# A gated mix of linear attention and a GEGLU MLP: loads, sums and products put in another order in four places, and one tile for four short-lived buffers

## The chip, the cores and the metric

The kernel runs on one core of one Trainium2 chip. The metric is the time of one execution on the device in microseconds (us), taken as the median of several runs.

## The reference

With `S` = 2048 tokens, `D` = 576, 32 heads of 18 and `Df` = 4608:

```python
g = sigmoid((x * gate_w).sum(-1))                      # one gate for each token
q, k, v = split(x @ wqkv)                              # 32 heads
phi = lambda t: where(t > 0, t + 1, exp(t)) + 1e-6
kv = einsum("bhsd,bhse->bhde", phi(k), v)              # sums over all tokens
z  = phi(k).sum over tokens
a  = (phi(q) @ kv) / (phi(q) @ z + 1e-6) @ wo          # linear attention
b  = (gelu(x @ w_gate) * (x @ w_up)) @ w_down          # MLP
out = g * a + (1 - g) * b
```

All of it is fp32. The keys' states `kv` need every token before the first query can be used, and the MLP needs nothing of the attention.

## The kernel before, in words

TensorE (PE) takes an fp32 operand as a rounded high part and the rest, the low part; a product is the sum of three matmuls: high by high, high by low and low by high. ACT writes high parts (a copy into `fp32r`), DVE or GpSimd (POOL) write low parts (a subtraction). The order of the instructions on each engine is written out by hand: nothing is scheduled by a planner, and an engine takes its instructions strictly in that order. The program has three stages.

**Keys and values** (L160 to L415). `w_first` and `x_first` (L168 to L186) issue the first loads of the weights `wkv` and the tokens `xt`, on ACT's queue and on SP's (SyncE's). For each of 16 token tiles `t` and three chunks `c` of the columns, `proj_mm` (L196) issues 14 matmuls for the projection, and `kv_post` (L210) forms phi(k) and v from it. `kv_state` (L242) adds tile `t`'s part to the states: for each of five groups of heads one matmul with the high part of v (L248, 252 columns, 144 for the last group) and one with the low part (L250, 126 columns, 72 for the last), ten in all. In the loop at L379 the states of tile `t-2` follow chunk `c` = 0 of tile `t`.

**Mixing** (L400 to L675). The order is written as words, and `run` calls them one by one. A letter names a step, the digits its token block `b` (of 512 tokens) and group, tile or index. `Q` is a query projection (L433, 14 matmuls of 512 columns), `a` its activation, `h` and `d` the parts for the denominators and their matmul (L570), `r` the reciprocals of a block (L592: for each half one ACT copy L598, one DVE addition L599 and one DVE reciprocal L600, then DMAs that spread them over the partitions). `p` scales the queries of one token tile (L615 DVE, L616 ACT, L617 and L618 DVE), `m` multiplies them with the combined weights (L628, 28 matmuls of 288 columns into one of two PSUM pairs), and `e` scales the pair by the gate on ACT and stores it (L633, L635). `X` loads a chunk of the MLP's tokens (L641; chunks 1 and 2 from POOL's queue), `y` forms four sums of its quarters in place (L645 to L648, DVE), and `Y` splits them into parts (L652 ACT, L655 POOL, four subtractions). `W` loads a whole set of MLP weights. In the last of the words the MLP's first products begin: `G1`, `G6`, `G2`, `G7`, each 14 matmuls there, with `g` for what follows them.

**MLP** (from L682). It is a Winograd-Strassen product: seven products for each of gate (G1 to G7) and up (U1 to U7) instead of eight, on 2x2 blocks of 256 features and 1024 tokens, so 2 passes over the tokens by 18 feature blocks: 36 periods. One G or U is 7 matmuls of 512 columns (L690). The down products D (`unit`, L781) are 6 matmuls of 288 columns (L787), each reading one feature operand (h or hx: A11, A12, A22, S1 to S4, with a high and a low half), and E (`unit_out`) adds their results into `sums`. The table `ORDER` (L39) is the order of one period, and `emit` (L929) goes through it for every period `p`; a mark of +1 means that the step belongs to the period before, and @ that POOL does it. When the sums of a group of four token tiles are complete, `gated` (L774) multiplies them with one minus the gate and adds the attention's part: ACT L776, then POOL L777. The last period has no next one to hide under: its down products are formed directly, 12 matmuls for each of 8 token tiles (`down`, L981), in the order 4, 5, 6, 7, 0, 1, 2, 3, and `down_out` (L992) adds each to `sums` and stores it.

Four buffers of the MLP, `p1`, `u2`, `u3` and `e0`, are tiles of a pool `mid` (L675), opened after the pool `chunks` of X's tiles is closed, so that they lie on memory that chunks had. `p1` takes the copy (L703, ACT) of product G1's bank, that is, of PSUM.

Of the kernel before, what the change touches and what calls it, by code (L numbers as in the profile page):

```python
# [21 lines left out]
NG = 5  # L22
# [28 lines left out]
def tile_gated_mix(ctx, tc, xt, xs, wkv, wq, wo, wgu, wgt, wdn, cst, out):  # L51
# [124 lines left out]
    x_first(nc.sync, 0)  # L176
    w_first(nc.sync, 0, *cols[1])
    x_first(nc.sync, 1)
    w_first(nc.sync, 1, 0, KVC)
    x_first(nc.sync, 2)  # L180
# [14 lines left out]

    def proj_mm(t, c, out_t, ops):  # L196
        b, c0 = divmod(t * 128, BS)
        lo, n = CH[c]
        for k, (xa, i, r, rows) in enumerate(x_ops(b, c0, 128)):
            if k in ops:  # L200
                nc.tensor.matmul(out_t[:, :n], xa, kvw[i][:rows, r, lo:lo + n], start=(k == 0), stop=(k == 13))  # L201

    pk, vt = {}, {}
# [37 lines left out]

    def kv_state(t):  # L242
        p = pk.pop(t)[1]
        v = vt.pop(t)
        for g in range(NG):
            R, k = GR[g], slice(GO[g], GO[g] + GR[g])
            o = acc_a[:, g // 2, (g % 2) * 252:(g % 2 + 1) * 252] if g < 4 else acc_b[:, 0, :2 * R]
            nc.tensor.matmul(o, v[:, g * VW:g * VW + 128], p[:, :, k], start=(t == 0 and g in (0, 2, 4)),  # L248
                             stop=False, skip_group_check=True)
            nc.tensor.matmul(o[:R, :R], v[:, g * VW + 128:g * VW + 128 + R], p[:, 0, k], start=False,  # L250
                             stop=(t == NST - 1), skip_group_check=True)

# [126 lines left out]
    for t in range(2, NST):  # L379
        for c in range(3):  # L380
            ps = bank()
            proj_mm(t, c, ps, range(14))
            if c == (1 if t == 2 else 0):
                kv_state(t - 2)
            for part in (("k0",), ("k1", "s"), ("v",))[c]:
                kv_post(t, c, ps, part)
            do()
            if steps:
                steps.popleft()()
        if t == 3:  # L390
# [149 lines left out]
    def kw_load(g):  # L540
        kwr = kwr_of[g] = kwp.tile([128, D], F32, name="kwr", bufs=4)
        if g < 4:
            nc.sync.dma_start(kwr, kw_d[128 * g:128 * g + 128])
        else:
            for i in range(2):
                nc.sync.dma_start(kwr[64 * i:64 * i + 64], kw_d[512:])
# [32 lines left out]
    run("""  # L579
s Q24 a24 w1 i1 Q20 u z w2 i2 Q21 Q23 a21 o1 a20 h21 o2 w4 i4 f1 w0 i0 Q22 n f2 o4 a23 f4 h20 w3 i3 o0 Q30 f0  # L580
l1 l4 d20 v a22 o3 l0 f3 d21 Q33
    """)
# [75 lines left out]
    run("""  # L658
h22 d22 c1 Q32 l2 a30 h23 l3 d23 h24 X0 h30 d24 Q31 c4 a33 c2 r2 d30 a32 c0 a31 c3 h32 h31 Q01 a01 Q34 d31 h33
a34 Q00 p20 d32 Q04 h34 a00 d33 a04 p21 h00 m20 x Q02 y0 h01 d34 m21 Q03 r3 d00 h04 d01 a02 a03 h02 Q10 h03  # L660
d02 Q11 e20 d03 p23 m23 Y0 p22 a10 d04 e21 p31 m22 h10 e23 p30 X1 y1 r0 a11 m31 e31 Q14 e22 m30 Y1 a14 p33 h11
Q12 a12 d10 Q13 d11 e30 m33 p32 h12 d12 a13
    """)
# [254 lines left out]
    for word in ORDER.split():  # L918
# [3 lines left out]
        table.append((word[:-2] if shift else word, shift, nc.gpsimd if on_pool else nc.vector))  # L922
    assert sorted(name for name, _, _ in table) == sorted(ops)
    last_of = [[name for name, _, _ in table if name[0] == g][-1] for g in "GU"]

    done = {(name, 0) for name in ("G1", "gp1", "G6", "gu2", "G2", "gel0", "G7", "gu3")}
    after = deque()

    def emit(name, n, e):  # L929
# [62 lines left out]
    def down_out(t, turn, by_halves):  # L992
# [4 lines left out]
        else:  # L997
            nc.vector.scalar_tensor_tensor(a, pr[turn % 2][:, :, :288], gate[:, 1, st:st + 1], a, op0=mul, op1=add)
# [21 lines left out]
    for group in (order[:2],) + tuple((t,) for t in order[2:]):  # L1020
# [65 lines left out]
```

## Time and profile before

| | |
|---|---|
| time before, median of 3 runs | 1516.87 us (1516.15 to 1518.5) |
| the profiled execution, its own time | 1517.35 us |
| its span in the trace | 1515.6 us |
| outside the span | 1.75 us |
| busy share PE / DVE / POOL / ACT | 99% / 73% / 49% / 38% |
| mean granted clock of PE | 0.996 |

The span is the time from the first to the last recorded work; busy is the time in which an engine executes. Busy times of matmuls overlap by a little, since they are pipelined: a row's start and the next row's start are the safer pair. A row of a timeline gives the start, the busy time, the engine, the line and the operation, and in brackets the idle time ahead of it with what ended it. A row of the waits gives the engine's instruction, what it waited for, the total, the number of waits and the longest. A row of the windows gives the busy time of PE, PE's weight load, DVE, ACT and POOL with their instruction counts, then the granted clock (1.00 is full), the share of DMA time and GB/s.

### The profile page before, as it was taken

To read this page: it belongs to the slowest core of one execution; us is meant where nothing else is said; L and a number is where in the kernel's file an instruction comes from. 1 tells how busy PE (TensorE), PEld (TensorE's weight loads), DVE (VectorE), ACT (ScalarE), POOL (GpSimd) and SP (SyncE) were. 2 spreads that over 40 slices of the span, in tenths; PEclk is the share of its full clock that TensorE was granted. 3 is DMA by queue.
4 is the path that set the end of the run, shared out by engine and by line. 5 is a ranking of instruction groups with operands and counts; after the bars stand their busy time and mean duration, and the time that the engine had idled before them with its cause. 6 is when DMAs were issued, how large, how long until landed. Compare 5 with 4: busy or idle time off the path is not lost.

```text
span 1515.6 us, 21450 instructions
## 1 busy us (share of the span) xinstructions
PE 1497.4 (99%) x8181; PEld 1326.2 (88%) x8181; DVE 1107.5 (73%) x1690; ACT 577.6 (38%) x965; POOL 746.9 (49%) x710
## 2 busy tenths in 40 slices
PE   9999998999999999999999999999999999999998
PEld 8999888888888888888888888888888888888887
DVE  6534677378888888888878867777777777777776
ACT  6655755333434343434343323222222222222223
POOL 1473412177877877878867625233233232332323
PEclk9999999999999999999999999999999999999999
DMA  6676565656666766665566376334433344344441
GB/s 214 205 254 217 172 210 190 205 193 212 205 222 243 253 241 220 211 232 200 202 236 216 115 300 239 151 138 162 179 147 138 138 176 160 138 153 182 181 172 63
DMA packets 115748, 291.15 MB, mean 192 GB/s; under 512 B 6845, under 2 KB 87037, under 8 KB 105278
## 3 DMA queue, kind: packets, MB, share of 16 engines
q1 hardware_dynamic: 111834, 276.63, 51.7%
q10 hardware_dynamic: 3524, 11.06, 2.1%
q0 software_dynamic: 288, 2.10, 0.4%
q8 instruction: 64, 1.05, 0.3%
q14 instruction: 38, 0.31, 0.1%
HBM read 177.09 MB, written 112.68 MB: 191 GB/s over the span
## 4 chain that ended last, share of the span: by engine, by line
PE 93%; DMA 2%; DVE 1%; issue 1%; POOL 1%; ACT 1%; POOLq 0%; SPq 0%; DVEq 0%; ACTq 0%
PE bank L690 53%; PE pair L787 26%; PE bank L201 7%; PE pair L628 2%; PE bank L433 2%; PE pair L248 1%; DMA xo<-xop_d 1%; DMA raw<-wkv 1%; POOL xo L655 1%; DMA xc<-xs 0%; PE pair L989 0%; POOL sums L777 0%; PE bank L436 0%; PE pair L250 0%; PE den L570 0%
## 5 line engine op out<-in xcount | busy, mean ns | idle before, releaser
L709 DVE TENSOR_TENSOR sums<-pair,sums 128x576 f32<-128x576 f32 x474 | 354.6, 754 | 160.5 <-PE pair L787 148.5
L690 PE MATMUL bank<-xo,wg 128*128 128x512 f32 x1764 | 441.1, 393 | 5.2 <-ACT p L703 3.6
L690 PE MATMUL bank<-xo,wu 128*128 128x512 f32 x1764 | 430.3, 393 | 0.8 <-DVE p L709 0.8
L690 PEld LDWEIGHTS bank<-xo,wu 128*128 128x128 f32 x1764 | 323.8, 188 | 64.2 <-DVE p L709 1.2
L690 PEld LDWEIGHTS bank<-xo,wg 128*128 128x128 f32 x1764 | 323.0, 189 | 64.2 <-ACT p L703 4.0
L787 PEld LDWEIGHTS pair<-wd,h 128*128 128x128 f32 x1680 | 248.2, 189 | 17.3
L787 PE MATMUL pair<-wd,h 128*128 128x288 f32 x1680 | 259.2, 296 | 0.0
L787 PEld LDWEIGHTS pair<-wd,hx 128*128 128x128 f32 x1260 | 179.1, 189 | 9.3
L787 PE MATMUL pair<-wd,hx 128*128 128x288 f32 x1260 | 184.4, 295 | 0.0
L703 ACT ACTIVATE p<-bank 128x512 f32<-128x512 f32 x72 | 43.0, 597 | 353.9 <-PE bank L690 348.0
L853 POOL TENSOR_TENSOR wd<-draw,wd 128x432 fp32r<-128x432 f32 x68 | 75.1, 1123 | 190.8 <-ACT wd L703 190.8
L829 POOL TENSOR_TENSOR h<-e,h 128x512 fp32r<-128x512 f32 x70 | 96.3, 1375 | 140.6 <-ACT h L703 140.6
L829 POOL TENSOR_TENSOR hx<-e,hx 128x512 fp32r<-128x512 f32 x70 | 96.7, 1401 | 113.1 <-ACT hx L703 113.1
L703 ACT ACTIVATE h<-e 128x512 fp32r<-128x512 f32 x107 | 67.3, 629 | 210.9 <-DVE e L709 206.5
L845 POOL TENSOR_TENSOR work<-work 128x256 f32<-128x256 f32 x136 | 113.3, 843 | 5.3
L201 PE MATMUL bank<-kvw,xo 128*128 128x378 f32 (+5 forms) x560 | 106.4, 342 | 1.6 <-DVE kvw L82 1.0
L201 PEld LDWEIGHTS bank<-kvw,xo 128*128 128x128 f32 (+1 forms) x560 | 95.8, 190 | 6.9 <-DVE kvw L82 1.6
L709 DVE TENSOR_TENSOR u<-bank,p 128x512 f32<-128x512 f32 x72 | 49.6, 689 | 47.3 <-PE bank L690 32.2
L703 ACT ACTIVATE hx<-e 128x512 fp32r<-128x512 f32 x105 | 63.9, 626 | 36.2 <-DVE e L709 36.2
L709 DVE TENSOR_TENSOR e<-bank,e 128x512 f32<-128x512 f32 x106 | 72.5, 684 | 1.2
L703 ACT ACTIVATE wd<-draw 128x864 fp32r<-128x864 f32 (+1 forms) x35 | 32.7, 934 | 99.3 <-PE pair L787 99.3
L628 PE MATMUL pair<-kw,p 128*128 128x288 f32 x448 | 64.0, 304 | 3.1 <-ACT ga L633 3.1
(175 smaller groups left out, 1831.8 us busy)
## 6 DMA issues: line engine op xcount, KB each, us to landing
wg<-wp_d SPq DMA_DIRECT2D x17, 2240.0 KB
wu<-wp_d SPq DMA_DIRECT2D x17, 2240.0 KB
wp_d<-wg SPq DMA_DIRECT2D x16, 2240.0 KB
wp_d<-wu SPq DMA_DIRECT2D x16, 2240.0 KB
draw<-wdn SPq DMA_DIRECT2D x35, 576.0 KB
work<-wgu SPq DMA_DIRECT2D x34, 512.0 KB
xo<-xop_d SPq DMA_DIRECT2D x7, 1280.0 KB
wt_d<-tail_op SPq DMA_DIRECT2D x15, 448.0 KB
```

Source lines behind the costliest of these rows:

```text
L201: nc.tensor.matmul(out_t[:, :n], xa, kvw[i][:rows, r, lo:lo + n], start=(k == 0), stop=(k == 13))
L248: nc.tensor.matmul(o, v[:, g * VW:g * VW + 128], p[:, :, k], start=(t == 0 and g in (0, 2, 4)), stop=False, skip_group_check=True)
L433: nc.tensor.matmul(ps, qw[i][:rows, c:c + 128], xa, start=(k == 0), stop=(k == 13))
L628: nc.tensor.matmul(y[:, i, :288], pa, w[:, i * 288:(i + 1) * 288], start=(n == 0), stop=(n == 13))
L655: nc.gpsimd.tensor_tensor(xo[rows, S2 + k, lo], raw[rows, k], f32(xo[rows, S2 + k, kt]), OP.subtract)
L690: nc.tensor.matmul(ps, w_, x_, start=start and i == 0, stop=i == 6, skip_group_check=not start)
L703: nc.scalar.activation(o, i, AF.Copy)
L709: nc.vector.tensor_tensor(o, a, b, op)
L787: nc.tensor.matmul(pr[q][:, j, :288], h[:, hl, c], wd[:, b, wl], start=start and i == 0, stop=i == 2, skip_group_check=not start)
L829: op(name + "l", lambda n, e, a=a, f=src_of: e.tensor_tensor(hb[a][:, 1], f(), f32(hb[a][:, 0]), sub))
L845: op(f"{name}T{i + 1}", lambda n, e, o=o, a=a, b=b: e.tensor_tensor(o, a, b, sub))
L853: op(f"dl{x}{j}", lambda n, e, i=i, src=src, c=c: e.tensor_tensor(wd[:, i, 1, c], src[:, :, c], f32(wd[:, i, 0, c]), sub))
```

## The change

Seven edits go together.

1. At the start, one load of weights (`w_first(…, 1, …)`, 1154 columns) goes to POOL's queue instead of SP's, where it stood between two loads of tokens.
2. `kv_state` becomes `kv_sums`: for `t` from 3 to 15 the ten matmuls of the states are put one by one behind the first ten of the 14 matmuls of chunk `c` = 0, the five with the high part first. The three other states (after `t` = 2 and at the end) come in one piece, with the five high ones first too.
3. The pool `mid` goes; one tile `spare` in a pool of its own is opened ahead of the mixing stage. Its slices are first the four buffers `kwr` of `kw_load`, and later `p1`, `u2`, `u3`, `e0`. `chunks` is closed later.
4. The words of mixing are put in another order.
5. The order in the table differs in three periods: in period 0 U4 stands ahead of U3, in period 18 (the first of the second pass) G4 ahead of G2; in the last period the steps dlt0, dlt1, S3h and S3l stand ahead of D10, and the down products run in the order 2, 7, 4, 1, 6, 5, 3 in place of 2, 1, 6, 5, 3, 7, 4.
6. `gated` is queued for each token tile as soon as its own sums are complete, where before four were queued together.
7. The last store of the output is made in two halves.

The core of the diff:

```diff
     w_first(nc.sync, 0, *cols[1])
+    w_first(nc.gpsimd, 1, 0, KVC)
     x_first(nc.sync, 1)
-    w_first(nc.sync, 1, 0, KVC)
...
-            proj_mm(t, c, ps, range(14))
-            if c == (1 if t == 2 else 0):
-                kv_state(t - 2)
+            proj_mm(t, c, ps, range(14), kv_sums(t - 2) if t > 2 and c == 0 else ())
+            if t == 2 and c == 1:
+                kv_state(0)
...
+    spare = base.pool("spare").tile([128, 4 * D], F32, name="spare")
+    p1, u2, u3, e0 = (spare[:, i * BS:(i + 1) * BS] for i in range(4))
...
-        kwr = kwr_of[g] = kwp.tile([128, D], F32, name="kwr", bufs=4)
+        i = len(kwr_of) % 4
+        kwr = kwr_of[g] = spare[:, i * D:(i + 1) * D]
...
-h02 Q11 e20 d03 p23 m23 Y0 p22 a10 d04 e21 p31 m22 h10 e23 p30 X1 y1 r0 a11 m31 e31 Q14 e22 m30 Y1 a14 p33 h11
+h02 d02 m22 a10 a04 X1 d03 p31 h04 d04 Q11 p30 y1 e23 Q12 Q14 h10 m31 e22 m30 r0 d10 Y1 X2 a11 a12 a14 p32 e31
...
-W0 m32 p01 h13 d13 X2 h14 e33 e32 m01 p00 d14 y2 m00 r1 Y2
-    chunks.close()
-    mid = mlp.pool("mid", side="right")
-    p1, u2, u3, e0 = (mid.tile([128, BS], F32, name=n) for n in ("p1", "u2", "u3", "e0"))
-G1 G6 g1 G2 p02 e01 p03 e00 G7 g6 m02 e02 m03 g7 p10 m10 e03 p11 m11 W1 p13 e10 p12 e11 m13 g2 e13 m12 e12
+W0 p00 h14 e32 m33 p01 d13 m00 e33 y2 d14 r1 Y2 m01 G1 G6 g1 p02 e00 G2 G7 p03 m02 e01 m03 g6 g7 e02 p11 m11
+e03 W1 p10 m10 e11 p13 g2 m13 p12 e10 e13 m12 e12
+    chunks.close()
...
+    tables = {0: before(table, "U4", "U3"), NF2: before(table, "G4", "G2")}
+    for name in ("dlt0", "dlt1", "S3h", "S3l"):
+        last = before(last, name, "D10")
+    tables[LAST] = [(x[0] + turned[int(x[1])] + x[2:], s, e) if x[0] in "DE" and s == 1 else (x, s, e)
+                    for x, s, e in last]
...
-                    after.extend((n // NF2, t) for t in ts)
+                if key not in called and all((f"E{k}{t % 4 // 2}", n) in done for k in ENDS[t // 4]):
+                    called.add(key)
+                    after.append(key)
...
+        if by_halves:
+            for i in range(2):
+                nc.sync.dma_start(out_of(st)[:, i], a[:, i])
```

Where the change moves instructions, three places matter for what follows. A row gives the line, the operation, what it writes and reads, the shape, and a count; a line number is that of its own kernel. The first is ACT in mixing, around the reciprocals of block 0 (`rb<-den`). The stores `ga_d_87`, `ga_d_88` and `ga_d_90` belong to the steps e22, e23 and e31; `xo<-xc` is the split of a token chunk. Before:

```order
L598 ACTIVATE rb<-den 32x256 x2
L447 ACTIVATE r_1676<-bank 128x512
L448 ACTIVATE r_1676<-r_1676 128x512
L633 ACTIVATE ga<-pair,gate 128x576
L635 DMA ga_d_90<-ga 128x576
L633 ACTIVATE ga<-pair,gate 128x576
L635 DMA ga_d_87<-ga 128x576
L652 ACTIVATE xo<-xc 128x4x512
```

The same place after the change:

```order
L649 ACTIVATE ga<-pair,gate 128x576
L651 DMA ga_d_88<-ga 128x576
L575 ACTIVATE hl<-r_1680 128x512
L649 ACTIVATE ga<-pair,gate 128x576
L651 DMA ga_d_87<-ga 128x576
L614 ACTIVATE rb<-den 32x256 x2
L668 ACTIVATE xo<-xc 128x4x512
```

Before, the two reciprocal copies of block 0 stood ahead of the pair copies of e31 and e22 on ACT. Now e23 and e22 come ahead of them, and e31 behind.

The second place is PE in the keys' stage: chunk 0 of token tile 3 (`kvw_160`, `kvw_161`: high and low weights) and the states of tile 1 (`vt_239`). Before:

```order
L201 MATMUL bank<-kvw_160,xo 128x378 x7
L201 MATMUL bank<-kvw_161,xo 128x378 x7
L248 MATMUL pair<-pk,vt_239 128x252
L250 MATMUL pair<-pk,vt_239 126x126
L248 MATMUL pair<-pk,vt_239 128x252
L250 MATMUL pair<-pk,vt_239 126x126
```

After the change, the rows from the fourth matmul of the chunk on:

```order
L202 MATMUL bank<-kvw_160,xo 128x378
L256 MATMUL pair<-pk,vt_239 128x252
L202 MATMUL bank<-kvw_160,xo 128x378
L256 MATMUL pair<-pk,vt_239 128x144
L202 MATMUL bank<-kvw_160,xo 128x378
L253 MATMUL pair<-pk,vt_239 126x126
L202 MATMUL bank<-kvw_160,xo 128x378
L253 MATMUL pair<-pk,vt_239 126x126
```

The states' matmuls stood together behind the chunk, high and low in turn; now each stands between two matmuls of the projection, all the high ones ahead of the low ones.

The third place is ACT at the head of the last period. `h_3092` before and `h_3084` after are the high half of operand S3, `h_3090` and `h_3082` that of A11; `p_2798` before and the `spare` written from `bank` after are p1, the copy of product G1. Before:

```order
L703 ACTIVATE wd<-dsum 128x4x288
L703 ACTIVATE h_3090<-e_2801 128x512
L703 ACTIVATE hx_3094<-e_3089 128x512
L703 ACTIVATE p_2798<-bank 128x512
L703 ACTIVATE hx_3096<-e_3087 128x512
L703 ACTIVATE hx_3095<-e_2801 128x512
L703 ACTIVATE h_3092<-e_3088 128x512
```

After:

```order
L716 ACTIVATE wd<-dsum 128x4x288
L716 ACTIVATE h_3082<-spare 128x512
L716 ACTIVATE hx_3086<-e_3081 128x512
L716 ACTIVATE spare<-bank 128x512
L716 ACTIVATE h_3084<-e_3080 128x512
L716 ACTIVATE hx_3088<-e_3079 128x512
L716 ACTIVATE hx_3087<-spare 128x512
```

S3's high half moved two copies up, to the place right behind G1's copy. On PE the first down product behind G1, which read A11 before, reads S3 now.

More of the change, by code (lines that the diff above doesn't have):

```diff
@@ L193, in tile_gated_mix, with proj_mm @@
     kp = keys.pool("kp", bufs=2, side="right")
-    def proj_mm(t, c, out_t, ops):
+    def proj_mm(t, c, out_t, ops, between=()):
+        between = list(between)
         b, c0 = divmod(t * 128, BS)
@@ L201, in proj_mm @@
                 nc.tensor.matmul(out_t[:, :n], xa, kvw[i][:rows, r, lo:lo + n], start=(k == 0), stop=(k == 13))
+                if between:
+                    between.pop(0)()
     pk, vt = {}, {}
@@ L240, in kv_post, with kv_sums, one, kv_state @@
             nc.vector.scalar_tensor_tensor(pl, r, EPS, f32(ph), op0=OP.add, op1=OP.subtract)
-    def kv_state(t):
+    def kv_sums(t):
         p = pk.pop(t)[1]
         v = vt.pop(t)
-        for g in range(NG):
+        def one(g, low):
             R, k = GR[g], slice(GO[g], GO[g] + GR[g])
             o = acc_a[:, g // 2, (g % 2) * 252:(g % 2 + 1) * 252] if g < 4 else acc_b[:, 0, :2 * R]
[L248 to L251, printed above, removed]
+            if low:
+                nc.tensor.matmul(o[:R, :R], v[:, g * VW + 128:g * VW + 128 + R], p[:, 0, k], start=False,
+                                 stop=(t == NST - 1), skip_group_check=True)
+            else:
+                nc.tensor.matmul(o, v[:, g * VW:g * VW + 128], p[:, :, k], start=(t == 0 and g in (0, 2, 4)),
+                                 stop=False, skip_group_check=True)
+        return [lambda g=g, low=low: one(g, low) for low in (False, True) for g in range(NG)]
+    def kv_state(t):
+        for f in kv_sums(t):
+            f()
     first = [(t, c) for t in range(2) for c in range(3)]
@@ L402, in tile_gated_mix @@
     kvs.close()
+    base = Scope()
+    spare = base.pool("spare").tile([128, 4 * D], F32, name="spare")
+    p1, u2, u3, e0 = (spare[:, i * BS:(i + 1) * BS] for i in range(4))
     mixing = Scope()
@@ L579, in tile_gated_mix @@
     run("""
-s Q24 a24 w1 i1 Q20 u z w2 i2 Q21 Q23 a21 o1 a20 h21 o2 w4 i4 f1 w0 i0 Q22 n f2 o4 a23 f4 h20 w3 i3 o0 Q30 f0
-l1 l4 d20 v a22 o3 l0 f3 d21 Q33
+s w0 i0 u w1 i1 Q20 a20 z w2 Q21 n a21 Q22 o0 h20 a22 o1 i2 f1 f0 h21 w4 i4 h22 Q23 o2 f2 w3 i3 l0 d20 Q32 v
+a23 d21 a32 o4 f4 o3 Q24 d22 f3 l1 l4 h23 Q31 d23 Q00
     """)
@@ L658, in tile_gated_mix @@
     run("""
[L659 to L662, printed above, removed]
+c0 l2 a24 h24 d24 l3 X0 a31 r2 c4 c1 Q34 Q30 a00 c2 c3 Q01 a34 y0 Q33 a30 h31 Q03 a01 h30 Q02 d30 d31 p21 m21
+h32 d32 a33 p20 m20 x h33 h34 d33 a03 p23 h00 e21 p22 d34 Q13 Q10 r3 d00 h01 d01 h03 a02 Q04 m23 a13 Y0 e20
+h02 d02 m22 a10 a04 X1 d03 p31 h04 d04 Q11 p30 y1 e23 Q12 Q14 h10 m31 e22 m30 r0 d10 Y1 X2 a11 a12 a14 p32 e31
+p33 m32 h11 d11 h12 h13 d12
     """)
@@ L671, in tile_gated_mix @@
     run("""
-W0 m32 p01 h13 d13 X2 h14 e33 e32 m01 p00 d14 y2 m00 r1 Y2
+e30
     """)
-    chunks.close()
-    mid = mlp.pool("mid", side="right")
-    p1, u2, u3, e0 = (mid.tile([128, BS], F32, name=n) for n in ("p1", "u2", "u3", "e0"))
     PER = NST // NP
@@ L923, in tile_gated_mix, with before @@
     assert sorted(name for name, _, _ in table) == sorted(ops)
+    def before(t, a, b):
+        w = [x for x in t if x[0] == a][0]
+        t = [x for x in t if x[0] != a]
+        t.insert([x[0] for x in t].index(b), w)
+        return t
+    turned = {1: "7", 6: "4", 5: "1", 3: "6", 7: "5", 4: "3", 2: "2"}
+    tables = {0: before(table, "U4", "U3"), NF2: before(table, "G4", "G2")}
+    last = table
+    for name in ("dlt0", "dlt1", "S3h", "S3l"):
+        last = before(last, name, "D10")
+    tables[LAST] = [(x[0] + turned[int(x[1])] + x[2:], s, e) if x[0] in "DE" and s == 1 else (x, s, e)
+                    for x, s, e in last]
     last_of = [[name for name, _, _ in table if name[0] == g][-1] for g in "GU"]
+    ENDS = [[k for k in CHAINS if CHAINS[k][1] in c] for c in ((C11, C12), (C21, C22))]
+    called = set()
     done = {(name, 0) for name in ("G1", "gp1", "G6", "gu2", "G2", "gel0", "G7", "gu3")}
@@ L944, in emit @@
         if n in (NF2 - 1, LAST - 1):
-            for pair_of, ts in ((("E30", "E31"), range(4)), (("E40", "E41"), range(4, 8))):
-                if name in pair_of and all((x, n) in done for x in pair_of):
-                    after.extend((n // NF2, t) for t in ts)
+            for t in range(PER):
+                key = (n // NF2, t)
+                if key not in called and all((f"E{k}{t % 4 // 2}", n) in done for k in ENDS[t // 4]):
+                    called.add(key)
+                    after.append(key)
     for m in range(2):
@@ L957, in tile_gated_mix @@
                 mix_load(0, t)
-        for name, shift, e in table:
+        for name, shift, e in tables.get(p, table):
             emit(name, p - shift, e)
@@ L998, in down_out @@
             nc.vector.scalar_tensor_tensor(a, pr[turn % 2][:, :, :288], gate[:, 1, st:st + 1], a, op0=mul, op1=add)
-        nc.sync.dma_start(out_of(st), a)
+        if by_halves:
+            for i in range(2):
+                nc.sync.dma_start(out_of(st)[:, i], a[:, i])
+        else:
+            nc.sync.dma_start(out_of(st), a)
     left = {name for name, _, _ in table if name[0] in "dD" and (name, LAST - 1) not in done}
     for p in (LAST, LAST + 1):
-        for name, shift, e in table:
+        for name, shift, e in tables.get(p, table):
             n = p - shift
@@ L1026, in tile_gated_mix @@
     mlp.close()
+    base.close()
     fixed.close()
```

## The prediction

> **What bounds the kernel now.** The page's busy line comes first.
>
> ```profile
> PE 1497.4 (99%) x8181; PEld 1326.2 (88%) x8181; DVE 1107.5 (73%) x1690; ACT 577.6 (38%) x965; POOL 746.9 (49%) x710
> ```
>
> PE works nearly all of the span. The change takes no matmul away, so it can only gain PE's waits, matmuls that ran slower than others of their kind, and the ends of the program. The waits of PE by what ended them name the places; a row gives the total, the number, and the longest.
>
> ```profile
> PE bank L690 <- ACT p L703: 3.6, 1, 3.6
> PE pair L628 <- ACT ga L633: 3.1, 1, 3.1
> PE bank L690 <- DMA xo<-xop_d: 1.6, 1, 1.6
> ...
> PE pair L989 <- DVE sums L998: 1.4, 2, 0.7
> PE bank L201 <- DVE kvw L82: 1.0, 2, 0.7
> PE bank L690 <- DVE p L709: 0.8, 1, 0.8
> PE bank L201 <- ACT kvw L81: 0.6, 1, 0.6
> ```
>
> Each is a single place, not a cost of every period. The two largest lie where mixing passes into the MLP. PE's timeline there:
>
> ```profile
> 231.15 6.65 PE L628 MATMUL pair<-kw,p 128*128 128x288 f32 x28 [3.07 <-ACT ga L633]
> ...
> 245.01 3.87 PE L628 MATMUL pair<-kw,p 128*128 128x288 f32 x28
> ...
> 268.02 4.98 PE L690 MATMUL bank<-xo,wg 128*128 128x512 f32 x14 [3.60 <-ACT p L703]
> ...
> 295.23 3.38 PE L690 MATMUL bank<-xo,wg 128*128 128x512 f32 x14
> ```
>
> The same 28 matmuls take 6.65 us after the first wait and 3.87 later; the same 14 take 4.98 after the second and 3.38 later. The windows say why: the last three columns are the granted clock, the DMA share and GB/s.
>
> ```profile
> 230.00:232.00 2.00, 0.85 (x3) 0.85 (x4) 1.97 (x3) 1.60 (x3) 0.00 (x0) 0.58 0.07 18
> 268.00:270.00 2.00, 1.98 (x5) 1.59 (x6) 1.31 (x3) 1.23 (x2) 0.00 (x0) 0.50 0.31 94
> 892.00:894.00 2.00, 2.00 (x13) 1.78 (x12) 1.20 (x3) 1.04 (x3) 0.00 (x0) 1.00 1.01 425
> ```
>
> The granted clock falls to half behind each wait of over 3 us. So the two cost 3.07 + (6.65 − 3.87) + 3.60 + (4.98 − 3.38) = 11.05 us.
>
> **The seam: −10.5.** What PE waited for, on ACT:
>
> ```profile
> 228.81 0.38 ACT L598 ACTIVATE rb<-den 32x256 f32<-32x256 f32 x1 [5.58 <-DVE rb L599]
> ...
> 230.38 0.72 ACT L633 ACTIVATE ga<-pair,gate 128x576 f32<-128x576 f32 x1
> ...
> 267.37 0.60 ACT L703 ACTIVATE p<-bank 128x512 f32<-128x512 f32 x1 [5.90 <-POOL xo L655]
> ```
>
> and behind that, on DVE and in the chain of waits:
>
> ```profile
> 225.59 0.69 DVE L645 TENSOR_TENSOR xc<-xc 128x512 f32<-128x512 f32 x1 [1.71 <-DMA xc<-xs]
> ...
> 240.51 0.92 DVE L617 TENSOR_TENSOR p<-r,p 128x512 fp32r<-128x512 f32 x1 [0.81 <-ACT p L616]
> ```
> ```profile
> 219.40 6.10 DMA xc<-xs
> ```
>
> First wait: m30 needs the PSUM pair that e31 empties. e31 stood on ACT behind r0's second copy, which idled 5.58 us for DVE, and DVE stood in y1, which waited for chunk X1. The new words put e23 and e22 ahead of r0 on ACT, so m30's pair no longer hangs on DVE. Second wait: p1's copy found its memory still read by Y2's splits on POOL, since p1 lay on chunk memory. In `spare` it lies on kwr's, whose last reader (c3) comes tens of microseconds earlier; and G1 now stands behind m01. Both waits should go, and with them the slow matmuls.
>
> What is late next? m32 wants p32, which DVE forms behind y1 and r0. Before, the way from X1's landing (225.59) to the end of a low part of the tile scaled first (240.51 + 0.92 = 241.43) took 15.84; with X1's transfer, 6.10, and its issue that is about 22.3 us from the end of Y0. By my walk through the new words Y0 ends at about the start of m22, and PE has m22, m31, m30 (3 × 3.7), three queries (3 × 3.2) and about a microsecond of denominators in hand, some 21.3 us, and needs the low part only at its third matmul. So p32 comes between 0 and 2 us late; I take +0.5. Sum −10.5, bounds −11.05 and −9.
>
> **States between the projections: +0.6.** PE and its weight load (PEld):
>
> ```profile
> 84.70 0.28 PE L248 MATMUL pair<-pk,vt 128*128 128x252 f32 x1
> 84.83 0.23 PE L250 MATMUL pair<-pk,vt 128*126 128x126 f32 x1
> 84.89 0.33 PE L248 MATMUL pair<-pk,vt 128*128 128x252 f32 x1
> ...
> 85.73 6.46 PE L201 MATMUL bank<-kvw,xo 128*128 128x326 f32 x35
> ```
> ```profile
> 84.71 0.19 PEld L250 LDWEIGHTS pair<-pk,vt 128*126 128x126 f32 x1
> 84.83 0.19 PEld L248 LDWEIGHTS pair<-pk,vt 128*128 128x128 f32 x1
> 84.94 0.19 PEld L250 LDWEIGHTS pair<-pk,vt 128*126 128x126 f32 x1
> ...
> 85.62 0.14 PEld L250 LDWEIGHTS pair<-pk,vt 128*72 128x72 f32 x1
> 85.69 2.42 PEld L201 LDWEIGHTS bank<-kvw,xo 128*128 128x128 f32 x16
> ```
>
> Ten matmuls take 85.73 − 84.70 = 1.03 us. A low one streams for 0.06 (84.83 to 84.89), but loads of 128 columns follow each other at 0.11 to 0.12, and the load for a matmul begins only when the one ahead of it starts: 84.71 beside 84.70, and 84.83 beside 84.83. One load ahead, no more. A low matmul is then too short to cover the next load wherever it stands; a projection covers only the one load behind it, and has time to spare that nobody uses. So interleaving moves the uncovered 0.05 about and removes none. One thing is lost: the short load of 72 columns (85.62 to 85.69, 0.07) followed the last high matmul, whose 144 columns cover little; now a load of 128 columns follows it, some 0.05 more. 13 times 0.05 is +0.6. Bounds: if all ten are bound by loads, 10 × 0.115 − 1.03 = 0.12, or +1.6; if loads could run two ahead, the streams would bind: five high and five low, about 4 × 0.12 + 0.07 + 4 × 0.06 + 0.03 = 0.82, so −0.21 × 13 = −2.7.
>
> [...]
>
> **The start: −0.8.**
>
> ```profile
> 3.08 0.43 SPq L169 DMA_DIRECT2D raw<-wkv  x1
> ...
> 8.07 1.26 ACT L81 ACTIVATE kvw<-raw 128x704 fp32r<-128x704 f32 x2 [1.91 <-DMA raw<-wkv]
> ```
>
> ACT waits 1.91 for the second weights. Issued from POOL, idle there, they start earlier. At most all three L201 waits go (1.0 + 0.6 = 1.6); the last of them hangs on other weights, and transfers share the DMA engines. I take half, −0.8; at worst tokens slip by an issue slot of 0.43 (+0.5).
>
> **U4 and G4: −2.4.** In period 0, U4 fills the 0.8 in which U3 waited for a bank: −0.8, bounds 0 and −0.8. In period 18:
>
> ```profile
> 886.52 11.06 DMA xo<-xop_d
> ```
>
> G2 waits 1.6 for the token operand A12, back from DRAM at 886.52 + 11.06 = 897.58. G4 reads A22, which was issued before it; G4's 7 matmuls (3.38/14 × 7, about 1.6) cover the wait, if A22 is in. Seven such operands come one behind another at 425 GB/s (the third window); 1280 KB take 3.1 us, so A22 lands about 3 us earlier. −1.6, bounds 0 and −1.6.
>
> **The end: −1.6.**
>
> ```profile
> 1494.33 9.28 POOL L777 TENSOR_TENSOR sums<-sums,work 128x576 f32<-128x576 f32 x6 [3.01 <-ACT sums L776]
> ```
>
> The two waits for L998 sum to 1.4: `down_out` takes tiles 4 to 7 first, while POOL's six L777 came in the order of the fours. Now tiles 6, 7, 4, 5 are queued as their sums complete, so POOL is done with them sooner: −1.4, bounds 0 and −1.4. The halved store lets the last transfer start behind half of the last addition; I estimate −0.2.
>
> **A new wait in the last period: +2.4.**
>
> ```profile
> 1468.52 0.97 PE L787 MATMUL pair<-wd,h 128*128 128x288 f32 x6
> 1469.33 1.76 PE L690 MATMUL bank<-xo,wg 128*128 128x512 f32 x7
> ```
> ```profile
> 1468.71 0.60 ACT L703 ACTIVATE p<-bank 128x512 f32<-128x512 f32 x1 [2.90 <-PE bank L690]
> ```
> ```profile
> 1472.94 1.30 POOL L829 TENSOR_TENSOR h<-e,h 128x512 fp32r<-128x512 f32 x1
> ```
>
> Behind G1, PE takes D70 at 1468.52, which now reads S3. S3's high half stands behind p1's copy on ACT, and that copy needs G1's bank (1468.71). So S3h runs from 1469.3 to about 1469.85 and its low half on POOL, 1.30, until about 1471.2; D70's third matmul needs the low half. Its last four matmuls (0.81/6 × 4 = 0.54) end near 1471.75, and G5 starts there instead of at 1469.33: +2.4. All of PE's queue stands behind it. Bounds: 0, if the rest of the turned order returns it, and +2.4.
>
> **Sum:** −10.5 + 0.6 − 0.8 − 2.4 − 1.6 + 2.4 = −12.3. The profiled execution, 1517.35, becomes 1505.05; it was 0.48 above the median of the runs, so the forecast is **1504.6**.
>
> **The rivals.**
>
> *Loads run further ahead* (chance 0.18). The states cost −2.7 instead of +0.6: 1501.3. Against it, the load starts above; for it, before never showed a short matmul between long ones. [...]
>
> *The seam still waits* (0.14). The order there is all new, and p32 has no margin. A wait of 2.5 with a half clock behind it, priced by the first one (2.78), less the 0.5 counted: +4.8, 1509.4.
>
> *The last period's wait drops the clock* (0.11). PE is idle in two pieces, before D70 and in it, 2.4 us together; the clock was seen to fall after 3.07. It costs 2.8 more: 1507.4. [...]
>
> *Slower* (0.03). `spare` is one tile; if each slice's writer waited for readers of the other slices, every period would wait for p1, u2, u3 or e0. From 12.3/36 = 0.34 us in each of 36 periods it loses; a wait as long as G2's, 1.6, gives 36 × 1.6 = 58 us: 1562. Against it: the slices don't overlap, and waits go by what overlaps.
>
> *G4 doesn't do what it says* (0.04). If A22 is as late as A12, G4 waits the 1.6 itself: 1506.2.
>
> **How the numbers follow.** The forecast has 0.50. The range goes from 1499.0 (loads further ahead, and the bounds of the start and of the new wait) to 1510.0 (the seam's wait): it leaves out the slower case and the far ends of the others. About 0.2% (3 us) is what a measurement of this kernel can tell from no change; all cases but the slow one lie 7 us or more below 1516.87. Faster 0.95, same 0.02, slower 0.03.
>
> **What would show it.** Right: no wait of PE over 1 us between 215 and 320, and a granted clock of 1.00 there; ten states' matmuls that add 1.05 to 1.15 us to chunk 0; PE waiting some 2 us for POOL's S3 low half at the first down product of the last period; no wait for `xo<-xop_d`. Wrong: chunk 0 with its states shorter than before (loads run ahead), a half clock anywhere before the end, or PE waits repeated in every period.

## The result, and the profile after

The changed kernel takes 1504.35 us (median of 4 runs, 1503.57 to 1505.82), the kernel before 1517.07 beside it. The ratio is 0.9916 with a 95% interval of 0.9899 to 0.9934. The profiled execution of the changed kernel took 1504.92, its span is 1503.2: 12.4 less than the span before.

First the waits of PE in the changed kernel, to be held against the rows of before in the prediction:

```profile
PE pair L165 <- DVE xo L162: 1.5, 1, 1.5
PE pair L802 <- ACT h L716: 1.2, 1, 1.2
PE pair L802 <- POOL h L844: 0.8, 1, 0.8
PE bank L202 <- DVE kvw L82: 0.5, 2, 0.3
PE pair L1021 <- ACT h L716: 0.4, 1, 0.4
PE pair L1021 <- DVE h L722: 0.4, 1, 0.4
```

The two waits of over 3 us are gone, and so are those for the operand from `xop_d`, for DVE's p and for the sums. (The first row is the warm-up at the start, as before.) New are L802's two, which are one place, and L1021's two.

Where did the time come from? Both kernels issue the same number of matmuls, and at the ends of the stages the same ones have been issued. So the start of the same matmul in both traces tells how far ahead the changed kernel is: its lead. Six such marks on PE's timeline of before:

```profile
17.92 2.40 PE L201 MATMUL bank<-kvw,xo 128*128 128x378 f32 x12
...
272.84 22.55 PE L628 MATMUL pair<-kw,p 128*128 128x288 f32 x168
...
316.43 0.97 PE L787 MATMUL pair<-wd,h 128*128 128x288 f32 x6
...
904.25 1.75 PE L787 MATMUL pair<-wd,hx 128*128 128x288 f32 x12
...
1466.92 1.76 PE L690 MATMUL bank<-xo,wg 128*128 128x512 f32 x7
...
1495.85 3.65 PE L989 MATMUL pair<-wd,h 128*128 128x288 f32 x24
```

and the same six after:

```profile
16.72 3.09 PE L202 MATMUL bank<-kvw,xo 128*128 128x378 f32 x16
...
260.48 22.55 PE L644 MATMUL pair<-kw,p 128*128 128x288 f32 x168
...
303.42 0.97 PE L802 MATMUL pair<-wd,h 128*128 128x288 f32 x6
...
889.60 1.75 PE L802 MATMUL pair<-wd,hx 128*128 128x288 f32 x12
...
1452.26 1.76 PE L703 MATMUL bank<-xo,wg 128*128 128x512 f32 x7
...
1485.17 1.75 PE L1021 MATMUL pair<-wd,h 128*128 128x288 f32 x12
```

The lead is 1.20 us after the first weights, 12.36 behind the seam (the place where mixing passes into the MLP), 13.01 when the second period of the MLP runs, 14.65 in the first periods of the second pass, 14.66 at G1 of the last period, 10.68 at the start of the last down products, and 12.4 at the end. Ahead of the seam it is 1.07: the 1173rd matmul, with equally many of each length issued before it, starts at 213.07 before and at 212.00 after. So 11.29 were won at the seam, 0.65 between it and the second period, 1.64 where the second pass begins, and 1.72 behind the last product; 3.98 were lost at the head of the last period. All periods between are alike to 0.01 us.

At the seam PE now goes without a wait and at full clock:

```profile
229.60 7.63 PE L644 MATMUL pair<-kw,p 128*128 128x288 f32 x56
...
237.53 3.88 PE L644 MATMUL pair<-kw,p 128*128 128x288 f32 x28
...
254.03 6.61 PE L703 MATMUL bank<-xo,wg 128*128 128x512 f32 x28
```
```profile
220.00:240.00 20.00, 20.00 (x121) 17.86 (x120) 15.39 (x23) 14.01 (x22) 5.61 (x5) 1.00 0.56 177
240.00:260.00 20.00, 20.00 (x128) 18.62 (x127) 15.77 (x22) 8.24 (x12) 6.05 (x4) 1.00 0.77 247
```

The row at 254.03 holds G1, G6, G2 and G7 in one piece. (Each is 7 matmuls, in the seam as elsewhere, so a row of 14 there is two products; the words on the kernel before that give each of them 14 are wrong.)

The head of the last period is the one place that got worse. PE and ACT there:

```profile
1455.22 0.53 PE L802 MATMUL pair<-wd,h 128*128 128x288 f32 x2 [1.21 <-ACT h L716]
1456.58 1.33 PE L802 MATMUL pair<-wd,h 128*128 128x288 f32 x4 [0.82 <-POOL h L844]
1457.71 2.70 PE L703 MATMUL bank<-xo,wg 128*128 128x512 f32 x7
```
```profile
1454.06 0.60 ACT L716 ACTIVATE spare<-bank 128x512 f32<-128x512 f32 x1 [2.89 <-PE bank L703]
1454.55 0.62 ACT L716 ACTIVATE h<-e 128x512 fp32r<-128x512 f32 x1
```

p1's copy waits for G1's bank, S3's high half follows it, two matmuls of D70 wait for that and the other four for the low half on POOL. G5 starts 5.45 us after G1 where 2.41 was usual, and takes 2.54 to the next row (1460.25) where 1.6 is usual: in this execution the clock fell as well, to 0.57 in the window from 1456 to 1458.

### The profile page after: what moved, and what is told of

Same layout as the page of the kernel before. It is cut to its first block, busy times and chain, and to the rows that moved or that the text cites. A ratio compares the mean times of both kernels' runs of the same rounds, so it can differ in the third digit from the quotient of the medians.

```text
span 1503.2 us, 21460 instructions
## 1 busy us (share of the span) xinstructions
PE 1494.4 (99%) x8181; PEld 1323.6 (88%) x8181; DVE 1105.4 (74%) x1690; ACT 577.0 (38%) x965; POOL 747.0 (50%) x711
## 4 chain that ended last, share of the span: by engine, by line
PE 98%; DVE 1%; DMA 0%; issue 0%; SPq 0%; POOL 0%; ACT 0%; DVEq 0%; POOLq 0%
PE bank L703 53%; PE pair L802 26%; PE bank L202 8%; PE pair L644 4%; PE bank L448 3%; PE bank L451 1%; PE pair L1021 1%; PE pair L256 1%; PE den L586 1%; DMA raw<-wkv 0%; PE pair L253 0%; DVE bank L722 0%; PE pair L545 0%; DVE h L722 0%; PE pair L202 0%
## 5 line engine op out<-in xcount | busy, mean ns | idle before, releaser
L802 PEld LDWEIGHTS pair<-wd,h 128*128 128x128 f32 x1680 | 248.6, 189 | 19.9 <-ACT h L716 1.6
L802 PE MATMUL pair<-wd,h 128*128 128x288 f32 x1680 | 260.1, 297 | 2.0 <-ACT h L716 1.2
L722 DVE TENSOR_TENSOR spare<-bank,spare 128x512 f32<-128x512 f32 x216 | 148.3, 687 | 85.9 <-PE bank L703 70.9
L802 PEld LDWEIGHTS pair<-wd,hx 128*128 128x128 f32 x1260 | 179.1, 189 | 9.3
L802 PE MATMUL pair<-wd,hx 128*128 128x288 f32 x1260 | 184.4, 295 | 0.0
L716 ACT ACTIVATE spare<-bank 128x512 f32<-128x512 f32 x72 | 43.2, 599 | 354.1 <-PE bank L703 354.1
L202 PE MATMUL bank<-kvw,xo 128*128 128x378 f32 (+5 forms) x560 | 115.6, 347 | 0.5 <-DVE kvw L82 0.5
L716 ACT ACTIVATE h<-e 128x512 fp32r<-128x512 f32 x71 | 44.4, 625 | 170.3 <-DVE e L722 170.3
L844 POOL TENSOR_TENSOR hx<-spare,hx 128x512 fp32r<-128x512 f32 x35 | 45.4, 1297 | 108.8 <-ACT hx L716 108.8
L722 DVE TENSOR_TENSOR e<-bank,spare 128x512 f32<-128x512 f32 x107 | 73.1, 683 | 10.1 <-PE bank L703 8.9
L719 ACT ACTIVATE e<-e 128x512 f32<-128x512 f32 x108 | 65.5, 622 | 0.4 <-DVE e L722 0.4
L644 PEld LDWEIGHTS pair<-kw,p 128*128 128x128 f32 x448 | 60.6, 188 | 0.9
```

Of the source, the lines that this page charges most:

```text
L644: nc.tensor.matmul(y[:, i, :288], pa, w[:, i * 288:(i + 1) * 288], start=(n == 0), stop=(n == 13))
L716: nc.scalar.activation(o, i, AF.Copy)
L719: nc.scalar.activation(o, i, AF.Gelu_apprx_tanh)
L722: nc.vector.tensor_tensor(o, a, b, op)
L802: nc.tensor.matmul(pr[q][:, j, :288], h[:, hl, c], wd[:, b, wl], start=start and i == 0, stop=i == 2, skip_group_check=not start)
L844: op(name + "l", lambda n, e, a=a, f=src_of: e.tensor_tensor(hb[a][:, 1], f(), f32(hb[a][:, 0]), sub))
```

## The experiments

Twelve kernels were run, one of them the changed kernel once more. The kernel before ran with each set, with a median of 1517.11 in the first (the first four below), 1516.8 in the second (the next four) and 1515.83 in the third; a difference between sets should be read with that 1 us in mind. Stretches within a profile don't have this uncertainty.

**S3 ahead of p1's copy.** In the last period's table the four moved steps go ahead of gp1:

```diff
-        last = before(last, name, "D10")
+        last = before(last, name, "gp1")
```

> One edit against the changed kernel: in the last period S3h (with dlt0, dlt1, S3l) stands ahead of gp1 instead of ahead of D10. On ACT this swaps two rows only, p1's copy and S3's high half. Theory of the prediction (D70 waits because S3h is queued behind p1's copy): PE's waits of 1.2 us for ACT's h and 0.8 us for POOL's h at the first down product of the last period go, G5 starts 2.41 us behind G1's start instead of 5.45, and where a half clock followed it goes too: 3.0 to 4.0 us less than the changed kernel, 1500.4 to 1501.4. Rival (the wait is POOL's: S3's low half has other work ahead of it there, so only the 1.2 us of ACT goes): a wait for POOL's h of 0.8 us or more stays, 1502.5 to 1503.2.

Measured: 1501.45 (1500.99 to 1501.62), ratio to before 0.9896 (0.9882 to 0.9909). PE's timeline at the same place:

```profile
1452.77 1.76 PE L703 MATMUL bank<-xo,wg 128*128 128x512 f32 x7
...
1455.17 1.76 PE L703 MATMUL bank<-xo,wg 128*128 128x512 f32 x7
```

G5 starts 2.40 behind G1, and neither wait is left. Two rows swapped on ACT are worth 2.6 to 2.9 us, against 1504.0 and 1504.35 of the changed kernel. The wait was the place of S3h behind p1's copy, and POOL had nothing else ahead of S3's low half.

**The changed kernel once more**, with no edit.

> The changed kernel itself, unaltered, to see how its executions differ. [...] Rival (the half clock of the profiled execution is the same in all, and the spread of 1503.57 to 1505.82 is noise of the transfers): the clock is the same in all executions, the times spread without groups.

Measured: 1504.0 (1503.5, 1503.77, 1504.22, 1505.21). Its profile has the same two waits, 1.20 and 0.82, but the four matmuls behind the second take 0.63, and the windows show why (first the profile of the result, then this one; the granted clock is the third number from the right):

```profile
1456.00:1458.00 2.00, 1.42 (x5) 1.42 (x6) 0.00 (x0) 0.21 (x1) 2.00 (x3) 0.57 0.16 57
```
```profile
1456.00:1458.00 2.00, 1.18 (x7) 0.94 (x8) 0.07 (x1) 0.90 (x2) 2.00 (x2) 1.00 0.50 203
```
```profile
1457.90 1.79 PE L703 MATMUL bank<-xo,wg 128*128 128x512 f32 x7
```

G1 started at 1452.95 there, so G5 came 4.95 after it, 2.54 late, and the next products at the usual pace. The same wait costs 2.54 in one execution and 3.98 in another; the half clock makes 1.4 of it. Seven of the profiled executions have this wait. Two of them show the half clock there, the one of the result and that of the kernel without low matmuls (0.55 from 1451 to 1453); in the other five the wait costs 2.54 to 2.56. Of the eight executions of the changed kernel three took 1504.92 or more and five 1504.22 or less, while the five kernels without the wait spread over 0.26 to 0.63 us each. Which of the unprofiled executions had the half clock can't be told: one at 1503.5 shows a mean clock of 0.999, so the times do not split cleanly by that mean.

**The plain order in the last period.** No steps moved, down products in the order 2, 1, 6, 5, 3, 7, 4:

```diff
-    last = table
-    for name in ("dlt0", "dlt1", "S3h", "S3l"):
-        last = before(last, name, "D10")
-    tables[LAST] = [(x[0] + turned[int(x[1])] + x[2:], s, e) if x[0] in "DE" and s == 1 else (x, s, e)
-                    for x, s, e in last]
```

> Against the changed kernel, the last period takes the order of every other period: no step moved ahead of D10, down products in the order 2, 1, 6, 5, 3, 7, 4. Tokens are still queued one by one, and the halved last store stays. Theory (the turned order pays 3.0 to 4.0 us at its head and earns 1.4 at the end, since the tiles that are finished first come first): 1.6 to 2.6 less than the changed kernel, 1501.7 to 1502.7, and two waits of PE for L1030's sums of 0.7 each are back at the end. Rival (queuing token by token is enough for the end, the turned order earns nothing): 3.0 to 4.0 less, 1500.4 to 1501.4, and no such waits.

Measured: 1501.23 (1501.03 to 1501.29), 0.9895 (0.9881 to 0.9908). No wait for sums at the end. The rival holds: the turned order costs at its head and earns nothing at the end, where both kernels take 18.0 us from the first of the last down products to the end of the span (1503.2 − 1485.17, and 1499.5 − 1481.49 here).

**The states together again.**

```diff
-            proj_mm(t, c, ps, range(14), kv_sums(t - 2) if t > 2 and c == 0 else ())
-            if t == 2 and c == 1:
-                kv_state(0)
+            proj_mm(t, c, ps, range(14))
+            if c == (1 if t == 2 else 0):
+                kv_state(t - 2)
```

> Against the changed kernel, the states' ten matmuls stand together behind chunk 0 again, high and low in turn, as before the change. Theory of the prediction (weights are loaded one ahead, so interleaving hides none of the loads and adds up to 0.05 us a time): a period of three chunks and states takes 8.52 to 8.55 us instead of 8.57, and the kernel 0.3 to 0.6 us less: 1503.9, not separable from the changed kernel by its time. Rival (between projections the loads hide): the period takes 0.25 us more, the kernel 3.3 more, 1507.6.

Measured: 1504.15 (1503.27 to 1506.12), within the spread of the changed kernel. The period can be read from the first state matmul of a tile to that of the next: first the changed kernel with some of its low matmuls and its weight loads (PEld), then the kernel with the states together.

```profile
72.92 0.28 PE L256 MATMUL pair<-pk,vt 128*128 128x252 f32 x1
...
74.38 0.22 PE L253 MATMUL pair<-pk,vt 128*126 128x126 f32 x1
74.44 0.39 PE L202 MATMUL bank<-kvw,xo 96*128 96x378 f32 x1
74.67 0.23 PE L253 MATMUL pair<-pk,vt 128*126 128x126 f32 x1
...
81.49 0.28 PE L256 MATMUL pair<-pk,vt 128*128 128x252 f32 x1
```
```profile
74.39 0.19 PEld L202 LDWEIGHTS bank<-kvw,xo 96*128 96x128 f32 x1
74.49 0.19 PEld L253 LDWEIGHTS pair<-pk,vt 128*126 128x126 f32 x1
```
```profile
75.06 0.28 PE L256 MATMUL pair<-pk,vt 128*128 128x252 f32 x1
...
83.61 0.28 PE L256 MATMUL pair<-pk,vt 128*128 128x252 f32 x1
```

8.57 interleaved and 8.55 together; the means of eight periods are 8.563 and 8.547, so interleaving costs 0.017 a time, 0.2 in all. The theory holds and the rival, 0.25 more for the states together, doesn't. A low matmul and the projection behind it take 0.29 (74.38 to 74.67): the projection starts 0.06 after the low one and then needs 0.23, where it needs 0.18 behind a high one (73.04 to 73.22). Its load starts with the low matmul, at 74.39, and the load for the next low one at 74.49, behind the projection's own start: one load ahead, as before.

**No low matmuls**, to price one by itself:

```diff
-        return [lambda g=g, low=low: one(g, low) for low in (False, True) for g in range(NG)]
+        return [lambda g=g, low=low: one(g, low) for low in (False,) for g in range(NG)]
```

> The changed kernel without the low matmuls of the states: it leaves out the low part of v in the states. This prices a low matmul between projections. Theory (a low matmul takes the time of a weight load, 0.115 to 0.125, though it streams for 0.06): a period of three chunks and states takes 5 x 0.12 = 0.55 to 0.6 us less than 8.57, about 8.0, and the whole 8 to 9.5 us less (16 times). Rival (its load hides under the projection, and it costs what it streams): 5 x 0.05 = 0.25 to 0.3 less, about 8.3, and the whole 4 to 5 us less.

Measured: one execution, 1499.23. First state matmuls of two tiles:

```profile
69.75 0.28 PE L256 MATMUL pair<-pk,vt 128*128 128x252 f32 x1
...
77.76 0.28 PE L256 MATMUL pair<-pk,vt 128*128 128x252 f32 x1
```

The period is 8.00 in the mean of two: five low matmuls cost 0.563, 0.113 each. That is the spacing of the loads (0.11 to 0.12 in the kernel before), not the 0.06 that they stream. The whole became only 5 us shorter and not 8 to 9.5. That is the rival's number, but not for its reason: two new waits of PE for DVE, 1.37 and 1.26, stand at the stage's end, and this execution had the half clock in the last period.

**The pool alone**, in the kernel before: `spare`, its slices for kwr and for p1, u2, u3, e0, and nothing else.

> The kernel before with one part of the change: p1, u2, u3 and e0 are slices of spare, shared with kwr, and chunks is closed later. The words of mixing are the old ones. Theory (the second wait is p1's memory and nothing else): p1's copy follows G1, G2 starts about 3.7 us sooner and runs at full clock (1.6 more), the wait for ga of 3.1 us at m30 stays with its half clock: 5.3 less than before, 1511.8. Rival 1 (p1's copy is held by Y2's split on ACT and POOL as much as by memory, so the order has to change too): 1 us or less, 1516. Rival 2 (spare is treated as one tile and the MLP's periods wait): slower than before.

Measured: 1511.15 (1510.23 to 1512.68), 0.9965 (0.9951 to 0.9979).

```profile
230.90 5.51 PE L632 MATMUL pair<-kw,p 128*128 128x288 f32 x28 [2.95 <-ACT ga L637]
...
259.64 6.61 PE L691 MATMUL bank<-xo,wg 128*128 128x512 f32 x28
```

The wait at m30 is there, the wait at G2 isn't: the four products run in one piece. The memory owned the second wait, and no period of the MLP waits for another slice: PE's one wait that names `spare` is 0.8 us, once, as long as the one for p in period 0 before.

**The new words alone**: p1, u2, u3 and e0 on chunks' memory again, all else as changed.

```diff
+e30 W0 p00 h14 e32 m33 p01 d13 m00 e33 y2 d14 r1 Y2
+    chunks.close()
+    mid = mlp.pool("mid", side="right")
+    p1, u2, u3, e0 = (mid.tile([128, BS], F32, name=n) for n in ("p1", "u2", "u3", "e0"))
```

> The changed kernel without spare: p1, u2, u3 and e0 lie on the memory of chunks, as before the change; all else, the new words too, stays. Theory (order and memory each own one wait): no wait at m30, but p1's copy waits for the end of Y2's splits on POOL (260.3 in the changed kernel's profile), so G2 starts at about 261.0 instead of 257.3: 3.7 us, and up to 1.6 for a half clock; 1508.0 to 1509.7. Rival (the new order alone brings Y2 early enough): as the changed kernel, 1504.4.

Measured: 1509.21 (1508.59 to 1510.15), 0.9949 (0.9937 to 0.9962). PE and ACT:

```profile
260.46 5.07 PE L702 MATMUL bank<-xo,wg 128*128 128x512 f32 x14 [2.74 <-ACT p L715]
```
```profile
259.82 0.60 ACT L715 ACTIVATE p<-bank 128x512 f32<-128x512 f32 x1 [5.91 <-POOL xo L667]
```

No wait at m30, but p1's copy waits for POOL's splits and G2 for the copy. Each part of the change owns one of the two waits.

**The second weights on SP's queue again.**

```diff
-    w_first(nc.gpsimd, 1, 0, KVC)
     x_first(nc.sync, 1)
+    w_first(nc.sync, 1, 0, KVC)
```

> The changed kernel with the second load of weights on SP's queue again, where it was before the change. Theory (the start gained 1.2 us by that load alone: PE's 60th matmul came 1.20 us sooner): PE's waits for L81's and L82's weights are back with 1.6 us in all, the 60th matmul 1.1 to 1.3 later, the kernel 1505.5. Rival (the gain of the start hangs on chance in the transfers): the 60th matmul within 0.4 of the changed kernel's.

Measured: 1504.92 (1504.43 to 1505.08), 0.6 to 0.9 more than the changed kernel, and inside its spread. On ACT the wait is back:

```profile
7.97 1.26 ACT L81 ACTIVATE kvw<-raw 128x704 fp32r<-128x704 f32 x2 [2.09 <-DMA raw<-wkv]
```

and the matmul that starts at 16.72 in the changed kernel starts at 17.89. The load's queue is worth 1.17 there, and nothing of it is lost in the MLP: at the start of the second pass the lead over before is 13.45 here and 14.65 in the changed kernel.

**Periods 0 and 18 in plain order.**

```diff
-    tables = {0: before(table, "U4", "U3"), NF2: before(table, "G4", "G2")}
+    tables = {}
```

> The changed kernel with the plain order in periods 0 and 18: U3 ahead of U4, G2 ahead of G4; the last period keeps the changed order. Theory (each swap covered one wait of before): U3 waits about 0.8 us for a bank in period 0 again, G2 about 1.6 for A12 in period 18: 2.0 to 2.6 more than the changed kernel, 1506.3 to 1507.0. Rival (the new order of mixing moved these waits anyway, so that the swaps do nothing): no such waits, 1504.4.

Measured: 1505.85 (1505.69 to 1506.03), 1.5 to 1.85 above the changed kernel. Both waits are back:

```profile
PE bank L703 <- DMA xo<-xop_d: 1.6, 1, 1.6
...
PE bank L703 <- DVE spare L722: 0.8, 1, 0.8
```

**Gated tiles in fours**, with the plain order in the last period:

```diff
-            for t in range(PER):
-                key = (n // NF2, t)
-                if key not in called and all((f"E{k}{t % 4 // 2}", n) in done for k in ENDS[t // 4]):
-                    called.add(key)
-                    after.append(key)
+            for pair_of, ts in ((("E30", "E31"), range(4)), (("E40", "E41"), range(4, 8))):
+                if name in pair_of and all((x, n) in done for x in pair_of):
+                    after.extend((n // NF2, t) for t in ts)
```

> The changed kernel with the plain order in the last period and with the gated tiles queued in fours as before the change; the halved last store stays. It prices the queuing by tile. Theory (with tiles queued one by one POOL is through with them in time, whatever the order of the down products): two waits of PE for the sums of 0.7 each are back, 1.4 more than with the plain order alone, 1502.6. Rival (the waits had another cause, and the plain order with tiles one by one or in fours does alike): 1501.2.

Measured: 1502.49 (1502.34 to 1502.76), 1.26 above the plain order alone, which ran in another set. The waits for the sums return:

```profile
PE pair L1014 <- DVE sums L1023: 0.9, 2, 0.7
```

So these waits go by the queuing tile by tile, under the plain order of the down products too.

**The last store in one piece**, with the plain order in the last period.

> The changed kernel with the plain order in the last period and the last store in one piece. Theory of the prediction (the halves earn 0.2): the stretch from the last matmul's start to the end of the span is 4.2 instead of 4.03, 1501.4. Rival (the end became 0.8 shorter by the halves, as the two profiles of before and after have it: 4.96 and 4.18): 4.7 to 4.9, 1501.9.

Measured: 1501.73 (1501.62 to 1502.1), 0.5 above the same kernel with halves, which ran in another set. By the stretch that the expectation names, the rival holds: the last matmul's start is 4.76 from the end here, and 4.04 with halves.

The end can be read in each profile by two stretches, from the start of the first of the last down products to the start of the last matmul, and from there to the end of the span (us):

| kernel | down products | behind the last matmul |
|---|---|---|
| before | 14.79 | 4.93 |
| the pool alone | 15.41 | 4.72 |
| changed | 13.85 | 4.14 |
| changed, plain order in the last period | 13.97 | 4.04 |
| the same with tiles in fours | 15.41 | 4.05 |
| the same with the last store in one piece | 13.97 | 4.76 |

So queuing by tile is worth 15.41 − 13.97 = 1.44, and the halves are worth 4.76 − 4.04 = 0.72.

**Both costs taken back**: the plain order in the last period, and the states together.

> The changed kernel with the two parts taken back that cost it time: the plain order in the last period, and the states' matmuls together behind chunk 0. Theory (3.0 for the last period, 0.26 for the states: 13 times 0.02): 1500.9 to 1501.2, below every kernel so far, by little. Rival (the interleaved states free something that the period's length doesn't show): 1501.3 or more.

Measured: 1501.08 (1500.7 to 1501.15), 0.9900 (0.9884 to 0.9917). It has the lowest median of the twelve but `no_low`, which leaves work out; beside the plain order alone (1501.23) the difference is smaller than what can be told apart. The three kernels that lack the new wait and keep the rest of the end (S3 ahead, the plain order alone, and this one) are about 3 us faster than the changed one.

## Why the prediction was right, point by point

The forecast was 1504.6, the result 1504.35; the sum was −12.3, the span fell by 12.4. Part of that closeness is luck: the seam, the start and the states came out 0.8, 0.4 and 0.4 better than forecast, the last period 1.6 worse. And one of the prediction's own signs of being wrong was there, a half clock before the end.

**The seam: forecast −10.5, measured −11.3** (the lead of 12.36 behind it, less the 1.07 ahead of it). Both mechanisms are shown, each by a kernel that has only the other part. Two things were mis-sized. The rows' idle times count from the modelled end of a matmul, which lies some 0.16 behind the start that the next one could have had:

```profile
226.77 1.31 PE L436 MATMUL bank<-xo,qw 128*128 128x512 f32 x5
```

Five matmuls at 0.23 (the five ahead of them start at 225.62, 1.15 earlier) from 226.77 end their turn at 227.92, and the next started at 231.15: 3.23 lost where the row says 3.07. G2 likewise lost 268.02 − (261.05 + 14 × 0.23) = 3.75 for 3.60. With the slow matmuls that makes 3.23 + 2.78 + 3.75 + 1.60 = 11.36, close to the 11.29 gained. And p32 was in time:

```profile
235.67 0.69 DVE L633 TENSOR_TENSOR p<-r,p 128x512 fp32r<-128x512 f32 x1 [0.87 <-ACT p L632]
```

Its low part ends at 236.36 and m32 starts at 237.53 without a wait. The +0.5 was not needed; the margin is 1.2 us. (The time in hand was added up wrong, too: 3 × 3.7, 3 × 3.2 and a microsecond are 21.7, not 21.3.)

**The states: forecast +0.6, measured +0.2.** The mechanism held: one load ahead, 0.113 for a low matmul between projections. The chance of 0.18 on loads further ahead fell with it. In the traces of before and after, none of the 8181 loads starts ahead of the start of the matmul before its own.

**The start: forecast −0.8, measured −1.2**, and 0.9 to 1.2 over the profiles of all kernels that have the load on POOL's queue; the bound of 1.6 was not reached. Half was too careful.

**U4 and G4: forecast −2.4, measured −2.3** by place. G4's 1.64 meets the forecast; in the profiles of the other kernels it is 1.40 to 1.77. U4's first gain is 1.0 (the same matmuls in the changed kernel and in the one with the plain order), but 0.4 of it is lost again at the first products of the next period; 0.65 stays. In the second profile of the changed kernel a wait of 0.7 for weights stands there, and only 0.1 stays.

**The end: forecast −1.6, measured −1.7**, and its parts were wrong in two ways that cancel. Tile by tile was 1.44 (forecast 1.4) and the halves 0.72 (forecast 0.2, an estimate with no row behind it). Some 0.4 of these 2.16 was lost again, in new waits of PE of 0.8 that the prediction did not see. They come from one subtraction on DVE; DVE and POOL in the changed kernel:

```profile
1483.57 1.66 DVE L722 TENSOR_TENSOR h<-e,h 128x512 fp32r<-128x512 f32 x1
```
```profile
1481.84 2.84 POOL L1009 TENSOR_TENSOR wd<-draw,wd 128x576 fp32r<-128x576 f32 x2 [22.85 <-issue]
```

and the same subtraction of before, on DVE:

```profile
1494.25 0.68 DVE L709 TENSOR_TENSOR h<-e,h 128x512 fp32r<-128x512 f32 x1
```

It took 0.68 when it began just ahead of POOL's work (1494.33), and 1.66 when it began behind POOL's: it ends at 1485.23, 0.55 behind POOL's instruction (1484.68), which is about what it takes by itself. All that follows on DVE, and the last operands that PE waits for, come 1 us later. No kernel was made to test that POOL holds DVE up, but the profiles at hand agree: in each of the other thirteen profiles this subtraction begins with POOL at work, and takes 1.65 to 1.77. The last such subtraction takes 1.30 in the changed kernel, with POOL at work, and 0.69 with the plain order in the last period, where POOL is idle from 1484.33 to 1485.67:

```profile
1488.52 1.30 DVE L722 TENSOR_TENSOR h<-spare,h 128x512 fp32r<-128x512 f32 x1
```
```profile
1484.96 0.69 DVE L722 TENSOR_TENSOR h<-spare,h 128x512 fp32r<-128x512 f32 x1
```

The prediction's step that the end only gains failed there. It is not the new order that does it: the pool alone keeps the end of before and has such waits too, of 0.6 and 0.3, with 15.41 for its down products in place of 14.79.

**The last period: forecast +2.4, measured +2.54 without the half clock and +3.98 with it.** The step was right to 0.15. The rival of a half clock, at 0.11, came true in the profiled execution and in two of seven profiles in all, at 1.4 and not 2.8: that price was taken from the matmuls behind the wait of 3.07, and those behind the wait of 3.60 had lost 1.6. The forecast should have carried it as a part of the sum.

**A22 in time, and spare by slices**: both rivals fell, shown by 1.64 at the second pass and by the pool alone.

**The range.** Its low end doesn't follow from the terms that it names: 1501.3 − 0.8 − 2.4 is 1498.1, not 1499.0.

By place the lead gives −1.20 at the start, +0.13 from there to the seam (the states among it), −11.29, −0.65, −1.64, +3.98 and −1.72, together −12.4; as differences of one lead they must add up.

## What to carry to other kernels

Before a step is moved to the head of a period, look at what stands ahead of it in its own engine's queue: S3's high half was ready to be formed, and a copy that waits for PE stood before it; two rows swapped gave back 2.6 to 2.9 us. Each of two stalls at one seam can have its own cause (an order on ACT, and memory shared with a reader on POOL), and a kernel that has only one of the edits shows which. And interleaving short matmuls with long ones hid no weight load here, where loads ran one ahead (8.563 us a period interleaved, 8.547 together); read the weight load's own timeline before counting on it.

## What the runs showed of the hardware that was not expected

- PE ran slow after a shorter wait than in the kernel before. Behind a wait of 2.74 us in the kernel with the new words alone, 14 matmuls took 5.07 in place of 3.38; before, the same 14 took 4.98 behind a wait of 3.60, at a granted clock of 0.50. And in two profiles of seven the granted clock fell, to 0.57 and 0.55, after waits of 1.2 and 0.8 with two matmuls between; in the changed kernel once more it stayed at 1.00 after waits of 1.20 and 0.82. No run here shows what decides between the two.
- A DVE subtraction with both operands in SBUF took 1.66 in place of 0.68 when a POOL subtraction was under way at its start: it ended at 1485.23, 0.55 behind POOL's end at 1484.68. One with an operand in PSUM (`h<-bank,h`, at 1486.55 in the changed kernel) took 0.68 with POOL at work.
